# A fused attention and matrix-product kernel: the planner's list scheduling by due times replaced by a listed order of 2706 tasks

## The chip, the cores and the metric

One NeuronCore of a Trainium2 chip. Its engines are TensorE (PE; PEld is its weight load), VectorE (DVE), ScalarE (ACT), GpSimd (POOL) and SyncE (SP). Each takes its own instructions strictly in the order in which the program lists them, and waits on semaphores for the others. In this program SP and POOL issue the DMAs. The metric is device time in microseconds, the median of several runs.

## The reference

Softcapped attention of 4 batches by 12 heads, then four weight matrices:

```python
def _attn_ref(q, k, v, cap):                      # (4, 12, 448, 64) each
    scores = scale * np.matmul(q, k.transpose(0, 1, 3, 2))
    scores = cap * np.tanh(scores / cap)
    scores = scores - np.max(scores, axis=-1, keepdims=True)
    attn = np.exp(scores)
    attn = attn / (np.sum(attn, axis=-1, keepdims=True) + 1e-09)
    return np.matmul(attn, v)

def _moe_ref(x, w1, w2, w3, w_out):               # x (1792, 768), d_ff 1024
    a = x @ w1
    b = x @ w2
    h = a * b @ w3
    return h @ w_out
```

`x` is the attention's output, laid out as 1792 tokens by 768. The weights arrive as 64-bit floats.

## The kernel before

**How the work is cut.** The 48 heads are 24 pairs. For a pair `pr` there are three score tasks `S{pr}_1..3` (L501, six matmuls each), and for each two pairs a fourth, `S{pr}_0` (L488, the last 64 keys, on 64x64 tiles of the array). Behind each stands a tanh `H` (L514) and an exp `E` (L517) on ScalarE. `V{pr}_1..3` (L555, four 32-column tiles) and `VJ` (L571, 64x64 tiles) multiply by v; `A` adds exps on VectorE (L621, L623); `T` and `Y` (L638, L651) sum with a matrix of ones. `Q` and `O` copy sums and values out of PSUM (L700, L704), and `R0` to `R3` invert the sums by way of DRAM, `N0` scales and `N` stores the pair's result (L744, L747).

All matmul operands but those of V, T and the 64x64 tasks are split in a high and a low part, each product being three matmuls. A weight piece goes through `load`, `low`, `sign`, `top`, `join` (64-bit to 32-bit on ScalarE and VectorE: L280 or L275, L286, L270 or L263, L291), then `high` and `out` or `h` and `l`: a rounding cast on either engine (L297, L341) and a subtraction on VectorE (L300, L344). `h{pr}_0` and `l{pr}_0` do this for q and k (L447, L451).

`O` and `Z` pieces are w_out and w3. `C` (pc, L1233) forms w3 @ w_out, evacuated by `D` and stored by `DS`. `W` pieces are w1 and w2, combined by a seven-product scheme (L362, L876), their splits stored by `WS` (L905) for a second use. `X` tasks load, combine and split the attention's output (tiles x0T, x0B, x1T, x1B). `P` (pab, L1098, three matmuls of 448 columns) are the products with w1 and w2; `eM1`, `eU`, `eM5`, `eV` copy them from PSUM (L1067), other `e` tasks combine them (L1078), `U` stores a * b (L1084). In the last part `q` loads those, `s`, `ha`, `la` combine and split them (L1363, L1384, L1388), `p` (m, L1452, 384 columns) multiplies with w3 @ w_out, and `w` stores the result (L1497).

**The two parts.** All tasks of the first part (24 pairs, w_out, w3, w1, w2, half of the products) are put into a plan and run; then the attention's pools are closed, and a second part is planned in the freed space. Its first tile that needs that space is written by `X1_0_0h`, a cast on ScalarE.

**What sets the order.** `put` gives a task its engine, an estimated duration, a due time (key), its needs, and for casts, evacuations and some loads and stores a second engine (ACT or DVE; SP or POOL). `Plan.run` then builds the program: it repeatedly takes the engine that is free first, takes from its ready tasks the one with the smallest due time, and emits that task's instructions; an estimated price is charged when a matmul task leaves one tiling of the array (`form`: S, Q, T or none) for another. `SHIFTS` moves the due times of 670 tasks by hand-listed amounts. The order of emission is each engine's order, and it also decides which buffer of a pool a tile gets, since pools hand out their buffers in turn. Estimated times take no part on the chip: semaphores alone do.

A second copy of the program, for a cap above 32, is built behind a branch; with the reference's cap of 30 it is not run.

Of the kernel before, what the change touches and what calls it, by code (L numbers as in the profile page):

```python
# [37 lines left out]
class Slots:  # L38
# [9 lines left out]
    def close(self):  # L48
        self.uses[self.closed :] = sorted(
            self.uses[self.closed :], key=lambda x: (x[0] + x[2].shift, x[1])  # L50
        )
# [94 lines left out]
def program(  # L146
# [85 lines left out]
    def put(name, eng, ns, key, emit, needs=(), lat=0.0, alt=(), after=()):  # L232
# [725 lines left out]
    def plan_xprep(r):  # L958
# [54 lines left out]
        for kt in range(HX):  # L1013
# [19 lines left out]
        for kt in range(HX):  # L1033
# [484 lines left out]
    with tc.manual_schedule():  # L1518
# [82 lines left out]
ldv2:-27.24 h2_0:-53.64 l2_0:-89.4 ld3:-70.26 ldv3:-35.39 ld4:-54.83 ldv4:-11.34 ld10:13.08
h11_0:36.3 ld13:-4.51 h13_0:45.03 ld14:-12.57 h14_0:31.49 ld15:-21.06 h15_0:31.8 ld16:-26.21
h16_0:21.8 ld17:-29.77 h17_0:19.68 l17_0:-10.19 ld18:-23.1 h18_0:20.3 ld19:-49.03 h19_0:16.53
ld20:-27.06 h20_0:7.2 ldv21:38.57 h21_0:35.19 ld22:-35.21 ldv22:37.84 h22_0:68.74 ldv23:38.58
h23_0:66.31 S0_1:-192.79 H0_1:-187.63 E0_1:-55.03 S0_2:-186.95 H0_2:-147.89 E0_2:-137.57
S0_3:-148.33 H0_3:-146.59 S0_0:-185.75 H0_0:-120.74 E0_0:-75.64 S1_1:-143.99 H1_1:-57.11
S1_2:-127.09 H1_2:-54.85 S1_3:-128.32 H1_3:-15.3 Q0:-49.46 O0:-18.46 N00:-29.44 T1:2.67
S2_1:-82.53 S2_2:-127.98 S2_3:-84.68 S2_0:-88.56 H2_0:4.61 S3_1:-80.27 H3_1:7.89 S3_2:-74.1
S3_3:-63.27 H3_3:7.08 V2_1:-4.66 VJ3:-3.79 V3_1:18.59 Q3:-1.56 S4_1:-56.06 H4_1:4.39 S4_2:-47.38
H4_2:7.21 S4_3:-34.57 H4_3:3.21 S4_0:-40.96 E4_0:-32.07 S5_1:-34.49 S5_2:-27.33 S5_3:-15.47  # L1610
# [48 lines left out]
X0a10:-52.7 X0t10:-19.82 X0c00:-15 X0b10:-18.2 X0T30:1.52 X0_5_0h:24.07 X0a11:-20.2 X0c01:3.2
X0_1_1h:22.17 X0_2_1h:-32.27 X0T31:-3.78 X0_5_1l:-13.29 X0a12:-3.41 X0t12:-2.26 X0b12:-3.23  # L1660
X0T22:13.58 X0_4_2h:24.23 X0_4_2l:13.95 P0_0_0_1:16.8 P0_0_0_2:-2.08 eM1_0_0:-47.62
P0_0_1_1:-24.42 eU_0_0:-6.02 P0_0_4_0:80.3 eV_0_0:-13.5 P0_0_5_0:12.86 P0_1_2_0:13.26
eU_0_1:-17.16 P0_1_3_0:6.71 eV_0_1:-31.07 P0_1_5_0:4.02 P0_2_0_1:2.93 P0_2_1_0:-2.97
# [105 lines left out]
```

## Time and profile before

| | |
|---|---|
| median of 3 runs | 565.93 us (565.09 to 569.05) |
| the profiled execution | 567.21 us, of which the span from first to last instruction is 565.4 us |
| TensorE | busy 548.5 us (97%), 3660 matmuls |
| VectorE | busy 433.0 us (77%), 874 instructions |
| ScalarE | busy 342.6 us (61%), 545 instructions |
| GpSimd | busy 82.1 us (15%), 150 instructions, nearly all DMA issues |
| DMA | 131.08 MB, 232 GB/s in the mean |

A row of the trace gives the line of the kernel, the engine, the operation, and the tile written and those read (`pab<-x0T,wt`), with buffer numbers left out. Matmuls overlap, and their ends are modelled: the distance between two starts or two ends in a full stretch is what one costs, not its own duration.

### The profile page before, as it was taken

Reading aid. Unit: us, or ns where it says so; the run is one execution under the profiler, and the core shown is the slowest. Engines: PE = TensorE matmul, PEld = TensorE weight load, DVE = VectorE, ACT = ScalarE, POOL = GpSimd, SP = SyncE. Lnnn points to the kernel's source line nnn. Section 1 sums busy time; section 2 is a strip of 40 time slices with the busy share of each in tenths; the row PEclk is TensorE's granted clock in tenths of the full one; section 3 lists DMA queues with packets and bytes.
Section 4 is the critical chain, followed back from the end, with each engine's and each line's share of the span. In section 5 each row is a group of like instructions: output and inputs, shape, how many; then the busy total and the mean of one; then the engine's idle time right before and its main releaser. Section 6 shows DMA issues by size and latency. Waiting matters only on the chain.

```text
span 565.4 us, 10168 instructions
## 1 busy us (share of the span) xinstructions
PE 548.5 (97%) x3660; PEld 426.7 (75%) x3660; DVE 433.0 (77%) x874; ACT 342.6 (61%) x545; POOL 82.1 (15%) x150
## 2 busy tenths in 40 slices
PE   6999999999999999999999899999999999999994
PEld 3354558977576556667578889899999999999994
DVE  5998999687989999998987898765522676875531
ACT  6998998487978999887854654422211353344120
POOL 0000011101131111212213120111011001111311
PEclk9999999999999999999999999999999999999998
DMA  8678777758897876977579877899886233553311
GB/s 277 172 254 277 240 233 252 244 182 261 283 329 261 272 255 236 353 254 290 197 271 348 321 253 245 274 340 300 295 291 261 89 108 102 179 148 107 85 70 64
DMA packets 62510, 131.08 MB, mean 232 GB/s; under 512 B 12738, under 2 KB 40770, under 8 KB 60914
## 3 DMA queue, kind: packets, MB, share of 16 engines
q1 hardware_dynamic: 51746, 78.65, 44.2%
q0 software_dynamic: 10704, 51.68, 24.3%
q8 instruction: 31, 0.51, 0.4%
q14 instruction: 29, 0.24, 0.1%
HBM read 88.46 MB, written 41.77 MB: 230 GB/s over the span
## 4 chain that ended last, share of the span: by engine, by line
PE 73%; issue 9%; DVE 7%; DMA 5%; ACT 3%; POOL 1%; SPq 0%; POOLq 0%; DVEq 0%; ACTq 0%
PE pab L1098 35%; PE m L1452 13%; PE pv L555 7%; PE s L501 6%; PE pc L1233 6%; DMA r<-r_dr 3%; PE sum L638 2%; DMA r_dr<-z 1%; PE s L488 1%; PE pv L571 1%; PE sum L651 1%; ACT p L514 1%; POOL out_dram L1497 1%; DVE wt L344 1%; ACT p L517 1%
## 5 line engine op out<-in xcount | busy, mean ns | idle before, releaser
L517 ACT ACTIVATE p<-p,ncap_sb,acap_sb 128x896 f32<-128x896 f32 x84 | 92.6, 1138 | 0.1
L514 ACT ACTIVATE p<-s,tsc_sb 128x896 f32<-128x896 f32 x84 | 82.3, 1008 | 8.8 <-PE s L501 5.9
L1233 PEld LDWEIGHTS pc<-wo,w3t 128*128 128x128 f32 x384 | 65.6, 188 | 12.1 <-issue 5.9
L1233 PE MATMUL pc<-wo,w3t 128*128 128x384 f32 x384 | 73.3, 342 | 0.4 <-DVE wo L300 0.4
L1098 PE MATMUL pab<-x0T,wt 128*128 128x448 f32 x288 | 64.8, 371 | 2.4 <-ACT M L1067 2.3
L501 PE MATMUL s<-hl 64*128 64x448 f32 x432 | 58.9, 396 | 5.7 <-ACT hl L447 4.4
L1098 PE MATMUL pab<-x1T,wt 128*128 128x448 f32 x288 | 63.5, 368 | 0.1
L501 PEld LDWEIGHTS s<-hl 64*128 64x128 f32 x432 | 38.0, 190 | 33.6 <-ACT p L514 9.9
L555 PE MATMUL pv<-p,v 128*32 128x448 f32 x576 | 62.6, 546 | 0.6 <-ACT p L517 0.4
L1098 PEld LDWEIGHTS pab<-x0T,wt 128*128 128x128 f32 x288 | 52.8, 188 | 13.5 <-ACT M L1067 3.4
L1452 PE MATMUL m<-bT,ot 128*128 128x384 f32 x336 | 61.9, 334 | 0.0
L1452 PEld LDWEIGHTS m<-bT,ot 128*128 128x128 f32 x336 | 58.6, 188 | 0.1
L1098 PEld LDWEIGHTS pab<-x1T,wt 128*128 128x128 f32 x288 | 53.9, 188 | 5.8 <-ACT U L1067 0.4
L1098 PE MATMUL pab<-x0B,wt 128*128 128x448 f32 x216 | 48.7, 370 | 0.0
L1098 PE MATMUL pab<-x1B,wt 128*128 128x448 f32 x216 | 48.2, 368 | 0.0
L1452 PE MATMUL m<-bB,ot 128*128 128x384 f32 x252 | 47.1, 334 | 0.0
L1098 PEld LDWEIGHTS pab<-x0B,wt 128*128 128x128 f32 x216 | 39.7, 188 | 7.2 <-issue 1.7
L1384 ACT CAST ot<-A 128x512 fp32r<-128x512 f32 x40 | 23.6, 621 | 35.1 <-DVE A L1363 27.7
L1452 PEld LDWEIGHTS m<-bB,ot 128*128 128x128 f32 x252 | 44.0, 188 | 0.0
L1098 PEld LDWEIGHTS pab<-x1B,wt 128*128 128x128 f32 x216 | 40.5, 188 | 4.1
L1067 ACT COPY M<-pab 128x448 f32<-128x448 f32 x27 | 14.3, 531 | 39.4 <-PE pab L1098 39.2
L555 PEld LDWEIGHTS pv<-p,v 128*32 128x32 f32 x576 | 15.5, 109 | 28.8 <-issue 18.6
(143 smaller groups left out, 801.7 us busy)
## 6 DMA issues: line engine op xcount, KB each, us to landing
raw_w<-in_moe_w_dram SPq DMA_DIRECT2D x48, 384.0 KB
w_dr<-wt POOLq DMA_DIRECT2D x42, 384.0 KB, 4.5
wt<-w_dr POOLq DMA_DIRECT2D x10, 1536.0 KB, 7.7
kq<-in_kq_dram SPq DMA_DIRECT2D x23, 450.0 KB
raw_wo<-in_moe_w_out_dram SPq DMA_DIRECT2D x16, 384.0 KB
A<-u_dr SPq DMA_DIRECT2D x24, 256.0 KB
v<-in_v_dram SPq DMA_DIRECT2D x24, 224.0 KB
r<-r_dr SPq DMA_DIRECT2D x48, 112.0 KB
```

What stands on the lines that cost most here:

```text
L344: nc.vector.tensor_tensor(dst(1), src(), dst(0), op=ALU.subtract)
L488: nc.tensor.matmul(box[0][quarter(pr + n, j), n, :S], lhsT=raw_t[pr + n][at, QO + S + KM :], rhs=raw_t[pr + n][at, QO : QO + S], start=Tru ...
L501: nc.tensor.matmul(box[0][:, j, :S], lhsT=hl[at, a, S + (i - 1) * P : S + i * P], rhs=hl[at, c, :S], start=(z == 0), stop=(z == 2),)
L514: nc.scalar.activation(p, box[0][:, :, :S], AF.Tanh, scale=tsc_sb)
L517: nc.scalar.activation(p_t[pr, i], p_t[pr, i], AF.Exp, scale=acap_sb, bias=ncap_sb)
L555: nc.tensor.matmul(pv_t[pr][n * 32 : (n + 1) * 32, :S], lhsT=v_t[pr][:, 3 * j + i - 1, g * 32 : (g + 1) * 32], rhs=p_t[pr, i][:, j, :], st ...
L638: nc.tensor.matmul(box[1][n * 32 : (n + 1) * 32, :SH], lhsT=ones[:, :32], rhs=part[:, j, g * SH : (g + 1) * SH], start=(x == 0), stop=(x = ...
L1067: cp(ev[name], box[bank][:, :S])
L1098: nc.tensor.matmul(box[bank][:, :S], lhsT=w_op(r, m, i)[:, a, kt, :], rhs=xt[r, i][:, kt, c, :S], start=(new and kt == 0 and z == 0), stop ...
L1233: nc.tensor.matmul(box[0][:, :NH], lhsT=w3t[n][:, a, jt, :], rhs=wo[jt][:, c, ns], start=(jt == 0 and z == 0), stop=(jt == KF - 1 and z == 2),
L1384: copy(ot[j][:, q % 3, 0], ru[src])
L1452: nc.tensor.matmul(box[banks[m]][:, :NH], lhsT=ot[q // 3][:, q % 3, a, k, :], rhs=bt[RHS[m]][:, k, c, :], start=(new and k == 0 and z == 0 ...
```

## The change

`Plan.run` no longer orders the main program. A text, `SEQUENCE`, names all 2706 tasks in order, 1663 before a bar and 1043 behind it (the planner of before put 1655 and 1051 into its two parts; the bar closes the attention's pools, as the end of the first part did). A name alone means the task's first engine; `/DVE`, `/ACT` or `/POOL` names its second. The tasks themselves, their instructions and their operands are the same. `SHIFTS` is removed. A need of one of the planner's tasks (T2) is corrected, for the general program, which alone is still planned.

```diff
-            self.uses[self.closed :], key=lambda x: (x[0] + x[2].shift, x[1])
+            self.uses[self.closed :], key=lambda x: (x[0], x[1])
...
-            t.key = (t.key + t.shift, i)
+            t.key = (t.key, i)
...
-    shifts = {} if general else {
-        x.split(":")[0]: float(x.split(":")[1]) for x in SHIFTS.split()
-    }
+    part = iter(SEQUENCE.split("|"))
+
+    def run(goals):
+
+        if general:
+            plan.run(goals)
+            return
+        for x in next(part).split():
+            name, _, eng = x.partition("/")
+            opts = done[name].opts
+            opts[eng or next(iter(opts))][1]()
...
-            total("T2", kt, "t1", "b1", "t1", key, [f"X{r}b1{kt}", f"X{r}T1{kt}" if r and kt else f"X{r}t1{kt}"])
+            total("T2", kt, "t1", "b1", "t1", key, [f"X{r}b1{kt}", f"X{r}_{op('T1')}_{kt}l" if r and kt else f"X{r}t1{kt}"])
...
-        plan.run(goals)
+        run(goals)
...
-SHIFTS = """
-ld0:-93.52 ldv0:-52.56 h0_0:-137.13 ld1:-66.82 ldv1:-42.73 h1_0:-55.2 l1_0:-66.93 ld2:-66.42
...
+SEQUENCE = """
+ld0 O0_0load ld1 O0_1load ldv0 ld2 O1_0load ldv1 h0_0/DVE l0_0 h0_1 cap S0_1 l0_1 H0_1 S0_2 O0_0low
+O0_0sign H0_2 O0_0top S0_3 O0_0join E0_1 h1_0/DVE O2_0load S0_0 O0_1low l1_0 H0_3 ld3 V0_1 O0_1top
...
+W6A11join P0_4_4_1 W6A21join W7A11load P0_4_4_2 N022 P0_4_3_2 N023 N22 eV_0_4 W5S4 N23 P0_4_6_0
+eM5_0_4 W6A12low/ACT P0_4_6_1 W5_5h W6A12sign P0_4_5_0 W6_0h/DVE W5_2l P0_4_6_2 W6S3 P0_4_5_1 |
+X1b00 X1a00 X1a02 WS5_3 X1a01 eu0_0_4 P0_4_5_2 W5_5l U0_4 P0_5_1_0 eo12_0_4 P0_5_1_1 X1b01 W6S1
+W7A12load P0_5_0_0 eo22_0_4 X1_0_0h WS5_4 W6A12top P0_5_0_1 WS5_2 W6_0l P0_5_0_2 W6S2 P0_5_1_2
+W6A12join eM1_0_5 X1_0_0l W7A11low/ACT P0_5_2_0 W6_2h W7A11sign P0_5_2_1 W6_3h eo11_0_5 P0_5_2_2
...
+p6_3_2 p6_6_3 p6_3_3 e6U p6_2_1 e612 p6_2_2 e6V w6o12 p6_4_0 e622 p6_2_3 p6_4_1 w6M5 e611/DVE
+p6_4_2 w6o11/POOL p6_4_3 e621 w6U
```

Against the order that the planner of before emits, task for task: 135 tasks move from ScalarE to VectorE and 69 the other way; 106 DMA tasks move from POOL to SP and 7 the other way. By engine, before and after: PE 876 and 876; VectorE 841 and 907; ScalarE 544 and 478; SP 303 and 402; POOL 142 and 43. The kind of tiling changes 156 times along the matmul tasks of before, 115 times along those of the list.

## Rows read from the trace of the kernel before

**Rows 1.** The page: busy us, share and instructions; busy tenths in 40 slices.

```profile
PE 548.5 (97%) x3660; PEld 426.7 (75%) x3660; DVE 433.0 (77%) x874; ACT 342.6 (61%) x545; POOL 82.1 (15%) x150
...
PE   6999999999999999999999899999999999999994
```

**Rows 2.** Stretches: us, busy us and instructions by engine, granted clock, DMA share, GB/s.

```profile
0.00:80.00 80.00, 74.32 (x672) 37.11 (x673) 67.98 (x165) 72.98 (x95) 3.03 (x9) 1.00 0.77 244
...
80.00:200.00 120.00, 118.16 (x919) 84.54 (x918) 106.89 (x225) 97.66 (x150) 20.39 (x37) 1.00 0.79 260
...
200.00:320.00 120.00, 118.44 (x832) 81.04 (x831) 108.59 (x214) 91.44 (x143) 24.96 (x42) 1.00 0.78 278
```

**Rows 3.** Chain that ended last: start us, us, engine, tile, line, instructions.

```profile
50.84 0.72 PE pc L1233 x3
...
54.79 1.14 PE sum L638 x24
...
89.62 17.90 PE pc L1233 x102
...
201.43 2.39 PE pv L555 x24
...
205.23 0.91 PE pv L571 x8
...
206.15 1.41 PE s L501 x12
...
207.55 0.81 PE pab L1098 x3
...
219.07 0.80 PE s L501 x6
...
226.96 0.89 PE pv L555 x8
...
358.83 92.02 PE pab L1098 x444
...
461.53 69.18 PE m L1452 x399
```

**Rows 4.** Timeline, first 30 us: start, us, engine, line, operation [idle before, releaser].

```profile
4.40 0.74 PE L501 MATMUL s<-hl 64*128 64x448 f32 x2 [4.40 <-ACT hl L447]
...
10.00 0.36 DVE L275 TENSOR_SCALAR raw_wo<-raw_wo 128x384 int32<-128x384 int32 x1 [2.97 <-DMA raw_wo<-in_moe_w_out_dram]
...
24.77 0.96 PE L555 MATMUL pv<-p,v 128*32 128x448 f32 x8 [0.45 <-ACT p L517]
```

**Rows 5.** Timeline, three later places where TensorE waited.

```profile
176.76 0.67 PE L501 MATMUL s<-hl 64*128 64x448 f32 x4 [1.04 <-DVE hl L451]
...
198.11 1.09 PE L1098 MATMUL pab<-x0T,wt 128*128 128x448 f32 x4 [0.77 <-ACT M L1067]
...
312.12 0.57 ACT L341 CAST x1B<-xs1a 128x448 fp32r<-128x448 f32 x1 [3.02 <-issue]
...
315.49 0.86 PE L1098 MATMUL pab<-x0T,wt 128*128 128x448 f32 x3 [1.54 <-ACT M L1067]
```

**Rows 6.** Lines by shape: count, busy us, mean ns, idle before.

```profile
L270 ACT ACTIVATE t_w<-raw_w 128x384 f32<-128x384 f32 x35 | 19.1, 561 | 0.3 <-DVE wt L344 0.2
...
L263 DVE TENSOR_SCALAR t_w<-raw_w 128x384 f32<-128x384 f32 x13 | 4.5, 349 | 0.0
...
L341 ACT CAST wt<-t_w 128x384 fp32r<-128x384 f32 x32 | 15.4, 512 | 10.5 <-DVE t_w L291 5.3 <-PE pab L1098 3.6 <-DVE t_w L362 1.5
...
L341 DVE CAST wt<-t_w 128x384 fp32r<-128x384 f32 x16 | 5.5, 350 | 0.5 <-PE pab L1098 0.5
```

**Rows 7.** DMA: the page's issues, lines by shape, SP's timeline and SP's waits.

```profile
w_dr<-wt POOLq DMA_DIRECT2D x42, 384.0 KB, 4.5
...
L905 POOL DMA_DIRECT2D w_dr<-wt x42 | 24.0, 571 | 80.2 <-DVE wt L344 64.3 <-issue 7.6 <-ACT U L1067 3.4
...
308.89 0.32 SPq L905 DMA_DIRECT2D w_dr<-wt  x1
...
SPq L1084 <- DVE M L1078: 35.4, 5, 20.1
```

**Rows 8.** Timeline, end of the span.

```profile
556.01 1.73 PE L1452 MATMUL m<-bB,ot 128*128 128x384 f32 x9
...
558.43 0.55 POOL L1497 DMA_DIRECT2D out_dram<-U  x1
```

More of the change, by code (lines that the diff above doesn't have):

```diff
@@ L1590, in program @@
             plan_out(t)
-        plan.run(goals)
+        run(goals)
 CAP_MAX = 32.0
-SHIFTS = """
-ld0:-93.52 ldv0:-52.56 h0_0:-137.13 ld1:-66.82 ldv1:-42.73 h1_0:-55.2 l1_0:-66.93 ld2:-66.42
[L1601 to L1610, printed above, removed]
@@ L1659 @@
[L1659 to L1663, printed above, removed]
-P0_2_4_0:4.59 P0_2_5_0:4.14 P0_2_6_0:-40.94 P0_3_0_0:2.54 P0_3_1_1:17.44 P0_3_2_0:2.86
@@ new lines @@
+S3_2 O2 ldv4 E3_1 R21 O2_1out T2 O4_0load Z0_2low O3_1high/DVE ld6 Z0_2top/ACT Y2 Z0_2sign H3_2
+O2_0out V3_1 N00 E3_3 S4_2 Z0_1high/DVE N0/POOL Z0_2join S4_1 O3_1out Q2 Z0_1out H4_2 R02 C0_1_2
+O3_0low O6_0load C0_0_1 O3_0top H4_1 O3_0sign R31 C0_0_2 O4_0top C0_1_3 E3_2 h5_0/DVE O3_0join S4_0
+O4_0low E4_2 O5_0load l5_0 S4_3 E4_1 O4_0sign V3_2 R12 H4_0 V3_3 O4_0join R22 O6_0low T3
+Z0_2high/DVE O3 N01 ldv5 Y3 O5_1load O6_0sign H4_3 N1/POOL V4_1 O6_0top h6_0/DVE Q3 S5_1 E4_3
+O6_0join R03 O3_0high/DVE S5_2 O4_0high/DVE O4_1load E4_0 O3_0out V4_2 R32 O5_0low O4_0out H5_2
@@ new lines @@
+V4_3 l6_0 ld7 O5_0top/ACT C0_0_3 O5_0sign E5_2 C0_0_4 O5_0join VJ5 R13 H5_1 O7_0load O5_1low R23
+S6_1 O4_1top O4 ldv6 O5_0high/DVE S5_3 E5_1 O4_1low O5_1sign T4 N02 O5_1top/ACT V5_1 N2 H5_3
+O5_1join O4_1sign V5_2 Z1_0load H6_1 O5_0out X0a00 Y4 h7_0/DVE E5_3 S6_2 O4_1join S6_3 Z0_2out
+O6_1load O5_1high/DVE H6_2 O7_0low V5_3 O5_1out Q4 O7_0sign E6_1 R04 S6_0 O7_0top ldv7 O6_0high/DVE
+O7_0join O5 ld8 T5 l7_0 E6_2 O7_1load Y5 R33 V6_1 Z1_0low H6_3 O7_0high/DVE O6_0out V6_2
+O4_1high/DVE H6_0 Z1_0top S7_1 O4_1out O6_1low/ACT Z1_0sign S7_3 O6_1top/ACT R14 Z1_0join E6_3
@@ new lines @@
+E13_3 Z7_1out R011 S14_1 ldv13 W0A12top R110 E13_2 S13_1 W0A12low R210 W1A12top C6_0_2 X0t10 W0S1
+Z7_2high H14_1 C6_1_2 W0S2 C6_0_3 Z7_2out W1A12low/ACT W0A12sign C6_1_3 h15_0 C6_1_4 W0A12join R310
+W1A12sign C6_0_4 H13_1 W1A11low C6_1_5 DS2_1 W1A12join C6_0_5 E13_1 R111 W1A22load C6_0_6 W1A11sign
+C6_1_6 W1A11top/ACT R211 W1A21load C6_0_7 W1A11join DS4_1 C6_1_7 W0_2h/DVE D6_0 A12_3 W0_6h VJ13
+X0_3_0h X0_3_0l V13_1 O12 D6_1 N010 X0b10 T12 X0_3_2h DS6_1/POOL W0_1h/DVE V13_2 ldv14 W1_1h A13_2
+Y12 X0_3_2l S14_3 Q12 W0_3h R012 A13_3 S14_2 X0c00 R311 h16_0 C7_0_0 l15_0 V13_3 H14_2 N10 W1A22low
@@ new lines @@
+W0_1l T13 H14_3 W1A22sign Y13 WS0_1/POOL l16_0 S14_0 W1_0h R112 S15_1 ld17 H14_0 W1_1l ldv15 C7_1_0
+N011 DS5_0 X0_3_1h C7_0_1 W2A11load W0_3l Q13 H15_1 R212 C7_1_1 X0T30 WS0_3/POOL N11 C7_0_2 X0_3_1l
+W1A21low/ACT R013 C7_1_2 W0S4 E14_1 X0c01 C7_0_3 X0T20 ld18 C7_0_4 W0_5h/DVE X0_1_0h W1A21sign
+C7_1_3 E14_2 X0_1_0l C7_1_4 X0_2_0h/DVE C7_0_5 W0_6l E14_3 C7_1_5 X0T40 C7_1_6 X0_2_0l O13 C7_0_6
+X0_4_0h A14_2 X0b11 C7_1_7 E15_1 R312 C7_0_7 X0_4_0l S15_2 D7_0 X0_5_0h/DVE X0a12 R113 E14_0 S15_3
+W1A21top R213 W0_2l V14_1 H15_2 X0_6_0h/DVE X0_6_0l V14_2 E15_2 X0_5_0l X0t11 V14_3 A14_3 X0a11
@@ new lines @@
+X0_5_1h WS1_1 VJ15 H15_3 W1A21join R313 X0T31 S16_1 O14 W0_5l WS0_2 E15_3 S16_3 W1A22top DS6_0 N012
+ldv16 T14 H16_1 V15_1 W2A12load A15_2 Y14 X0_1_2h V15_2 D7_1 A15_3 Q14 H16_3 V15_3 R014 X0T21 N12
+T15 X0_1_1h X0_5_1l Y15 X0_2_1h X0_1_1l S16_2 X0b12 X0_4_1h X0_2_1l E16_1 S16_0 X0_4_1l N013 h17_0
+X0t12 P0_0_0_0 W1S3 ldv17 P0_0_0_1 Q15 X0_1_2l H16_2 R015 P0_0_1_0 X0T41 WS0_0 P0_0_0_2 H16_0
+W2A12low X0c02 R114 P0_0_1_1 W1_0l eM1_0_0 R214 P0_0_1_2 l17_0 E16_0 ld19 P0_0_2_0 WS0_6 eo11_0_0
+W2A11low/ACT P0_0_2_1 X0T22 O15 P0_0_3_0 E16_3 R115 P0_0_3_1 W2A12sign R215 h18_0/DVE E16_2
@@ new lines @@
+X1_0_1h/DVE P0_5_3_2 W5_6l WS5_5/POOL W6_1l P0_5_4_0 eM5_0_5 X1_0_1l P0_5_4_1 W7A11top P0_5_4_2
+W6S4 W7A11join P0_5_5_0 eV_0_5 X1_0_2l W7A22load P0_5_5_1 W6_6h X1T12 W6_5h P0_5_6_0 W6_2l X1a10
+P0_5_5_2 W7A12low XT10 X1T11 P0_5_6_1 X1c00 eo12_0_5 P0_5_6_2 X1b10 W7A12sign WS5_6 P0_6_0_0
+eu0_0_5 WS6_1 W7A22top/ACT P0_6_0_1 X1_3_0h/DVE W7A22low/ACT W6_3l P0_6_0_2 W6_4l P0_6_1_0
+W7A12top/ACT eM1_0_6/DVE X1t10 W7A21top/ACT P0_6_1_1 eo22_0_5 WS6_0 W7A21low/ACT P0_6_1_2 W7A22sign
+eu1_0_5 P0_6_2_0 eo11_0_6 P0_6_2_1 U1_5 W7A12join P0_6_3_0 X1T30 P0_6_3_1 W6_5l X1_4_0h P0_6_3_2
@@ new lines @@
+P1_7_3_2 w1g1/POOL X1_6_2l P1_7_4_1 eM5_1_7 bT1_0 P1_7_4_2 bB11_1h X1_5_2l bT1_0h P1_7_5_0 bT3_0
+eV_1_7 X1_6_1l P1_7_5_1 bT3_0h P1_7_6_0 bT3_0l bT1_0l P1_7_5_2 bc11_2_0 bB11_1l P1_7_6_1 eo12_1_7
+P1_7_6_2 bT1_1 P1_0_0_0 eu0_1_7 bT1_1h P1_0_0_1 bT1_1l U2_7/POOL P1_0_0_2 bT2_1 w1g2/POOL bT2_0
+P1_0_1_0 eM1_1_0 bT3_1 P1_0_1_1 bT2_0h bc21_0_0 bc21_1_0 bT3_1h/DVE P1_0_1_2 bT3_1l P1_0_2_0
+eo11_1_0 P1_0_2_1 eo22_1_7 P1_0_2_2 P1_0_3_0 eU_1_0/DVE P1_0_3_1 eu1_1_7 P1_0_3_2 U3_7 P1_0_4_0
+eM5_1_0/DVE w1g3 P1_0_4_1 bc12_2_0 P1_0_5_0 P1_0_4_2 P1_0_5_1 eV_1_0 P1_0_5_2 bB11_2h P1_0_6_0
@@ new lines @@
+eo12_1_0 P1_0_6_1 bT2_1h/DVE P1_1_0_0 P1_0_6_2 P1_1_0_1 eu0_1_0 P1_1_0_2 eo22_1_0 U2_0/POOL
+P1_1_1_0 bT4_0 eM1_1_1 bT2_1l w1g4/POOL P1_1_1_1 bT2_0l P1_1_2_0 bT4_1 bc22_2_0 P1_1_1_2 q0A11
+P1_1_2_1 eo11_1_1 q0A21 P1_1_2_2 P1_1_3_0 eU_1_1/DVE P1_1_3_1 bB11_2l eu1_1_0 P1_1_4_0 P1_1_3_2
+U3_0 P1_1_4_1 bc21_2_0 eM5_1_1/DVE P1_1_4_2 bT1_2 bT4_0h/DVE P1_1_5_0 eV_1_1 w1g5 bT4_0l P1_1_5_1
+bT1_2h q0A22 eo22_1_1 bT4_1h P1_1_6_0 bT3_2 P1_1_5_2 bT3_2h P1_1_6_1 eo12_1_1 P1_1_6_2 bT1_2l
+P1_2_0_0 eu0_1_1 P1_2_0_1 bT3_2l U2_1 P1_2_1_0 bc11_3_0 P1_2_0_2 bc12_3_0 P1_2_1_1 eM1_1_2 P1_2_1_2
```

227 lines of the change are left out of this document (146 added, 81 removed).

## Prediction

> **What bounds the kernel now.** I read the page first, for the busy shares and the forty slices; then the stretches, to see whether one engine limits everywhere; then the chain of work that ended last, for the price of a matmul in a full stretch and just behind another kind; then the timeline where TensorE's idle time has a named releaser.
>
> The page says TensorE [rows 1]: 548.5 of 565.4 us busy, every slice but the first and last at 8 or 9 tenths, at a granted clock of 1.00 (2.4 GHz) in every stretch [rows 2]. Matmul ends are modelled, so "busy" hides two things the reader is to see: time lost in changing the tiling of the array, and short waits. The chain shows the first [rows 3]. A projection matmul (pab) in a run of 444 costs 92.02/444 = 0.207 us, but three behind another kind take 0.81, not 0.62: 0.19 for the change. Likewise: pc 17.90/102 = 0.1755, three behind another kind 0.72: 0.19. Scores (s): a second task of six adds 1.41 - 0.80 = 0.61, so the first carries 0.19. Values (pv): (2.39 - 0.89)/2 = 0.75 per task, the change 0.14. The 64x64 tasks always stand between other kinds (0.91); I take 0.17 of that, the mean of the other prices, an estimate.
>
> With these the time can be taken apart. TensorE runs from 4.40 us [rows 4] to 556.01 + 1.73 = 557.7 [rows 8]: 553.3 us. Matmuls alone: 1008 pab x 0.207 = 208.9; 588 m x (69.18/399) = 101.9; 384 pc x 0.1755 = 67.4; 72 score tasks x 0.61 = 43.9; 72 value tasks x 0.75 = 54.0; 480 sum matmuls x (1.14/24) = 22.8; 24 of the 64x64 tasks x 0.74 = 17.8. Together 516.7. In the order of before, the kind changes 156 times: 23 times into pc, 18 into pab (0.19 each), 43 into scores (0.19), 48 into values or sums (0.14), 24 into 64x64 (0.17): 4.4 + 3.4 + 8.2 + 6.7 + 4.1 = 26.8. The rest, 553.3 - 516.7 - 26.8 = 9.8 us, is waiting. Three waits of it lie late: 1.04, 0.77 and 1.54 [rows 5]; most of the others lie in the first 80 us, where ScalarE (72.98 of 80) and VectorE (67.98) are nearly full too [rows 2].
>
> So TensorE's own stream is the bound, and an order can win at most part of 26.8 + 9.8.
>
> **The change part by part.**
>
> *The order of the matmuls.* No matmul is added or removed. I counted the changes of kind along the listed tasks: 115 instead of 156. Into pc 13 (10 fewer), pab 10 (8 fewer), scores 39 (4 fewer), values and sums 32 (16 fewer), 64x64 21 (3 fewer): 1.9 + 1.5 + 0.8 + 2.2 + 0.5 = 6.9 us saved. All at 0.14 would be 5.7, all at 0.19 7.8: these are the bounds. 17 of the 41 lie among the first 100 matmul tasks (61 changes, now 44): 2.9 us in the first 80, 4.0 later. Value 6.9.
>
> *Casts moved from ScalarE to VectorE.* 135 tasks move there, 69 move back: net 66. A move is a piece's top from 561 to 349 ns, or a cast from 512 to 350 [rows 6], so ScalarE loses some 66 x 0.53 = 35 us of busy time and VectorE gains some 66 x 0.35 = 23. Early this matters. Up to the last exp of head pair 7, ScalarE's list shrinks from 88 to 79 tasks; beside tanh, exp and the two copies per pair it holds 10 instead of 18. That takes 8 x 0.5 = 4 us out of the engine for which values wait at 24.77. In the first microseconds h0_0 goes to VectorE ahead of the cap's scalars, and the first raw w_out load moves up from sixth to second on SP, so the 2.97 us that VectorE lost waiting for it falls away [rows 4]. Against that, VectorE takes the moved work where it has 12 us of 80 free. Between "the 4 us reach TensorE" (-4) and "VectorE is late instead" (+1.5) I take -1.2, nearer to nothing, because VectorE is at 85% there [rows 2].
>
> *The three late waits.* At 313 us: ScalarE stood in x1B's first cast (3.02 idle, then 312.12), the copy of M queued behind it, and TensorE waited for the copy [rows 5]. That cast writes a buffer whose space the attention pools hold until the last store of pair 23, which GpSimd issued. In the list N23 is issued by SP, and nine matmul tasks stand between it and that cast instead of seven (1.2 us more), so I expect the wait to shrink, not to go. At 176 us the scores of pair 15 waited for l15_0; four matmul tasks stand between them now, instead of two, but the sum T13 has only three behind its addition A13_3 instead of nine. At 198 us the copy eM1_0_0 was late; one matmul task stands behind it instead of none. Together 3.35 us; bounds -3.35 and 0; value -1.2, a third.
>
> *DMA issues.* 106 tasks move from GpSimd to SP and 7 the other way: SP issues 402 of 445 tasks instead of 303, GpSimd 43 instead of 142. An issue costs SP 0.32 us where it cost GpSimd 0.57 [rows 7]; SP gets 99 x 0.34 = 34 us more of issuing over 565, hidden since it feeds nothing but itself. What isn't hidden is order: on SP a store that waits for its data holds every load listed behind it. The price is with the rivals. At the end the last store, w6U, goes from GpSimd (issue 0.55, [rows 8]) to SP (0.32): -0.2, bounds 0 and -0.6.
>
> The Trainium skill, DMA: Bandwidth & Descriptors (Specifications), gives a first byte after about 1 us for GpSimd's path and 0.6 for SP's; by it N23 would land 0.4 us sooner. No row here shows a landing on SP's queue beside GpSimd's 4.5, so the sum stands without it.
>
> *What falls to nothing.* Sorting buffers and computing due times happen when the program is built; no instruction. The corrected need of T2 is read by the planner alone, which now runs only for the general branch; that branch is skipped at cap 30. If the cover failed it would cost that whole second program, which the trace of before doesn't run either.
>
> *New waits.* The stream gets 7 us shorter, so the other engines have that much less time, and VectorE goes from 106.9 and 108.6 busy of 120 [rows 2] to some 111 and 113. New short waits have no row; bounds 0 and +7 (all the saving refilled); I take +2.3, a third.
>
> **Sum.** -6.9 - 1.2 - 1.2 - 0.2 + 2.3 = -7.2 us. On the span: 565.4 to 558.2. The profiled execution took 567.2, 1.3 more than the median of 565.93, and would come to 560.0; the median to 558.7 us.
>
> **Rivals.**
>
> 1. *VectorE is the real limit up to 320 us.* For: 283.5 us busy of 320 [rows 2], 89%, and it gets some 6 us more of work there (566 tasks in the first part instead of 545). If its idle time stays what it is, the matmuls before 320 us, where every change of kind lies, can't come sooner, and only the last store and half a wait remain: -1 to -3, some 564 (the sum of half a wait, 0.8, the last store, 0.2, and up to 2 that VectorE's shorter idle time gives). Against: part of its idle time is waiting for others, such as the 2.97 us at the start [rows 4], and the list removes some of that.
>
> 2. *SP's queue holds the loads: slower.* For: before, SP already stood 35.4 us in five waits for u0's data, 20.1 in the longest [rows 7], and 67 of the moved tasks are stores of split weights, products and heads that will stand ahead of loads. If a weight or x load comes late by a landing, 4.5 us [rows 7], a whole row of matmuls waits. Two such cancel the gain; three make 558.7 + 13.5 = 572.2, slower by 1%. Against: stores stand in the list right behind what they store, so each waits briefly if that is on time, and loads are listed several tasks ahead. From the third held load on this decides.
>
> The Trainium skill speaks for this rival: Perfetto Trace Analysis (DMA Optimizations) advises balancing issues across engines and keeping inputs on one and outputs on another. The list does the opposite. That page's premise is a queue full of issuing; here 402 tasks at 0.32 us [rows 7] are 129 us, under a quarter of the span.
>
> 3. *The list is the old order in another form.* Excluded: 204 compute tasks and 113 DMA tasks change engine, and 41 changes of kind go.
>
> **How the numbers follow.** Forecast (shorter stream, about as much waiting): 0.61, own range 553.5 to 561. Rival 1: 0.29, 560.5 to 566. Rival 2 with a full price: 0.10, 566 to 580. A tenth of the forecast's share could fall below 553.5, when the waits go as well (-6.9 - 4 - 3.4 = 551.6). The range 553 to 566 leaves out about 0.06 below and 0.12 above. One per cent, about what a measurement of this kernel tells from no change, is 560.3 and 571.6. The forecast lies below 560.3 but for a small part (0.03): faster 0.58. Rival 1, that part and half of rival 2 lie within: 0.37. Slower: the other half, 0.05, the case of three held loads or more.
>
> **What the profile after would show.** GpSimd's busy time falls to 43 x 0.57 = 25 us, ScalarE's to about 308, VectorE's rises to about 456; 3660 matmuls as before. The first matmul starts within 0.5 us of 4.4, the last ends near 550. In the stretch 80:200 more matmuls fit than 919. If rival 1 holds, VectorE is over 95% busy up to 320 us and TensorE's waits name it. If rival 2 holds, TensorE or the casts wait for DMA loads and SP shows long waits at stores (L905, L747, L1084). Wrong would be: fewer changes of kind and yet the same length of stream before 320 us with no waits named, for then the price of 0.14 to 0.19 isn't one of the change.

## The result and the profile after

The changed kernel takes 552.21 us in the median (551.51 to 554.15, 4 runs), where the kernel before took 566.1 beside it: a ratio of 0.9752, 95% interval 0.9707 to 0.9797. A later comparison on one chip gave 553.03 us and 0.9733 (0.9703 to 0.9762). It is faster, by nearly twice what was forecast: 552.2, where 558.7 was expected and 553 was the lower end of the range. Its profiled execution took 551.55 us, its span 549.8 (before: 567.21 and 565.4). Line numbers of the new kernel are those of before plus 7.

The page, busy us by engine and the tenths of TensorE, beside [rows 1]:

```profile
PE 538.0 (98%) x3660; PEld 430.4 (78%) x3660; DVE 454.7 (83%) x940; ACT 310.6 (56%) x479; POOL 25.4 (5%) x49
...
PE   6999999999999999999999999999999999999995
```

As many matmuls as before, 10.5 us less busy time for them, no slice at 8 tenths any more between the first and the last. ScalarE lost 32 us, VectorE gained 22, GpSimd went from 82 to 25.

The same three stretches as [rows 2]:

```profile
0.00:80.00 80.00, 75.46 (x718) 41.83 (x718) 72.33 (x179) 72.90 (x92) 1.93 (x6) 1.00 0.77 245
...
80.00:200.00 120.00, 119.61 (x942) 86.88 (x939) 109.36 (x229) 100.69 (x151) 3.26 (x6) 1.00 0.82 257
...
200.00:320.00 120.00, 119.95 (x824) 88.38 (x822) 115.22 (x237) 84.15 (x135) 7.02 (x13) 1.00 0.85 294
```

TensorE stands 0.39 us in 80:200 and 0.05 in 200:320, where it stood 1.84 and 1.56. It does so although VectorE is 96% busy in the last of them. The waits of TensorE, in total, times, longest, are two:

```profile
PE s L508 <- DVE hl L454: 4.4, 1, 4.4
...
PE pab L1105 <- DVE M L1085: 0.4, 1, 0.4
```

The first is the wait for the first q and k; of the later waits only this one of 0.4 us is named.

**Where the time went.** To compare runs I took every trace apart in one way. For each matmul task the distance from its start to the next one's start is known; I subtracted the undisturbed distance of its kind (0.52 us for a task of pc or m, 0.62 for pab, 0.61 for scores, 0.75 for values and the 64x64 tasks, 0.38 for eight sum matmuls) and, at a change of kind, its price (the prediction's 0.14 to 0.19, parted into what comes before and behind the change). What is left is waiting. So the column of changes is a count times the prediction's prices and no measurement of its own; that the stretches without a wait come out near zero by them, and the fourth experiment, are what speaks for the prices. The tail is from the end of the last matmul to the end of the span. In us of the profiled execution (its own time is up to 2.2 us off its kernel's median):

| kernel | median | changes of kind | waits 0 to 80 | waits 80 to 320 | from 320 on | tail | span |
|---|---|---|---|---|---|---|---|
| before | 566.1 | 156: 26.4 | 6.0 | 4.6 | 0.6 | 7.6 | 565.4 |
| after | 552.21 | 115: 19.6 | 3.7 | 1.3 | -1.5 | 6.6 | 549.8 |
| after, once more | 553.03 | 115: 19.6 | 3.7 | 1.1 | 0.1 | 6.8 | 551.1 |
| issuers as before | 553.13 | 115: 19.6 | 4.1 | 1.8 | -1.5 | 7.3 | 551.4 |
| casts' engines as before | 562.14 | 115: 19.6 | 5.6 | 8.5 | -1.6 | 7.7 | 559.8 |
| start as before | 558.01 | 130: 22.2 | 5.1 | 4.0 | -1.3 | 6.7 | 556.9 |
| 24 changes more | 557.61 | 139: 23.9 | 4.0 | 1.2 | -1.6 | 7.2 | 554.6 |
| 135 casts to ScalarE | 569.50 | 115: 19.6 | 7.2 | 16.4 | -1.7 | 7.4 | 569.3 |
| 69 casts to VectorE | 560.69 | 115: 19.6 | 3.6 | 9.2 | 0.0 | 6.7 | 559.0 |
| 7 changes fewer | 558.51 | 108: 18.5 | 9.2 | 2.7 | 0.3 | 7.9 | 558.5 |
| 9 changes fewer | 564.09 | 106: 18.1 | 8.8 | 8.0 | -1.3 | 7.9 | 561.5 |
| before, list's issuers | 570.91 | 156: 26.4 | 6.2 | 7.5 | 3.6 | 7.4 | 571.2 |
| before, list's casts' engines | 579.59 | 156: 26.4 | 7.5 | 13.4 | 3.7 | 7.4 | 578.3 |
| before, list's start | 584.71 | 141: 23.7 | 4.1 | 25.8 | 2.9 | 7.7 | 584.1 |

The -1.5 is no wait: some executions ran pab faster there (last section). So I compare waits up to 320 us, and the whole by the second trace of after, whose pab runs as before's. There 14.3 us of span went, by this division: 6.8 with the changes of kind, 5.8 with waits before 320 us, 0.5 behind, 0.8 in the tail, 0.3 at the first matmul.

### The profile page after: what moved, and what is told of

Same layout as the page of the kernel before. It is cut to its first block, busy times and chain, and to the rows that moved or that the text cites. A ratio compares the mean times of both kernels' runs of the same rounds, so it can differ in the third digit from the quotient of the medians.

```text
span 549.8 us, 10088 instructions
## 1 busy us (share of the span) xinstructions
PE 538.0 (98%) x3660; PEld 430.4 (78%) x3660; DVE 454.7 (83%) x940; ACT 310.6 (56%) x479; POOL 25.4 (5%) x49
## 4 chain that ended last, share of the span: by engine, by line
PE 93%; DMA 3%; ACT 1%; DVE 1%; SPq 0%; issue 0%; ACTq 0%
PE pab L1105 37%; PE m L1459 19%; PE pc L1240 13%; PE pv L562 9%; PE s L508 9%; PE sum L645 3%; PE pv L578 2%; PE s L495 2%; PE sum L658 2%; DMA v<-in_v_dram 1%; DMA r_dr<-z 1%; ACT p L524 1%; DMA kq<-in_kq_dram 1%; DMA w_dr<-wt 1%; ACT p L521 1%; DVE M L1085 0%
## 5 line engine op out<-in xcount | busy, mean ns | idle before, releaser
L524 ACT ACTIVATE p<-p,ncap_sb,acap_sb 128x896 f32<-128x896 f32 x84 | 94.1, 1139 | 0.4
L1240 PE MATMUL pc<-wo,w3t 128*128 128x384 f32 x384 | 70.4, 339 | 0.0
L1459 PE MATMUL m<-bT,ot 128*128 128x384 f32 x336 | 67.8, 334 | 0.0
L508 PE MATMUL s<-hl 64*128 64x448 f32 x432 | 57.3, 393 | 4.4 <-DVE hl L454 4.4
L1459 PE MATMUL m<-bB,ot 128*128 128x384 f32 x252 | 52.4, 334 | 0.0
L1391 ACT CAST ot<-A 128x512 fp32r<-128x512 f32 x26 | 15.5, 621 | 38.5 <-DVE A L1370 20.9
L562 PEld LDWEIGHTS pv<-p,v 128*32 128x32 f32 x576 | 16.6, 109 | 24.2 <-issue 14.9
```

The lines of the kernel that those rows point to most:

```text
L508: nc.tensor.matmul(box[0][:, j, :S], lhsT=hl[at, a, S + (i - 1) * P : S + i * P], rhs=hl[at, c, :S], start=(z == 0), stop=(z == 2),)
L524: nc.scalar.activation(p_t[pr, i], p_t[pr, i], AF.Exp, scale=acap_sb, bias=ncap_sb)
L562: nc.tensor.matmul(pv_t[pr][n * 32 : (n + 1) * 32, :S], lhsT=v_t[pr][:, 3 * j + i - 1, g * 32 : (g + 1) * 32], rhs=p_t[pr, i][:, j, :], st ...
L1240: nc.tensor.matmul(box[0][:, :NH], lhsT=w3t[n][:, a, jt, :], rhs=wo[jt][:, c, ns], start=(jt == 0 and z == 0), stop=(jt == KF - 1 and z == 2),
L1391: copy(ot[j][:, q % 3, 0], ru[src])
L1459: nc.tensor.matmul(box[banks[m]][:, :NH], lhsT=ot[q // 3][:, q % 3, a, k, :], rhs=bt[RHS[m]][:, k, c, :], start=(new and k == 0 and z == 0 ...
```

## The experiments

Each kernel is the listed one, or the one before written as a list, with some tasks moved or given another engine; a task without a suffix has its usual engine. The edits are shown by their first tokens. Experiments 5 to 8 ran on another chip than 1 to 4 and 9 to 12; the kernel before took 566.1 to 567.4 us in the median in all of them, so amounts between kernels are good to about a microsecond.

**1. Issuers as before.** All 113 DMA tasks that changed queue go back.

```
-N2 N3 DS0_1 DS0_0 ... w6U
+N2/POOL N3/POOL DS0_1/POOL DS0_0/POOL ... w6U/POOL
```

> The listed order with the DMA issuers of before: 106 tasks back from SP to GpSimd and 7 from GpSimd to SP, each at its place in the list. Theory (the gain is 6.8 us of changes of kind and 7.6 us of waits, most of them VectorE's, ScalarE's and the first loads'): the issuer matters at two places alone, the store N23 before the second part's first cast (up to 1.5 us of waiting back) and the last stores (about 1 us): 552.9 to 554.7 us; no other named wait of TensorE. Rival (the issuer is what took the waits away): waits come back in many places, 556 to 560 us. Rival (SP's queue holds loads in the listed order): GpSimd's issuing makes it faster, under 551 us.

553.13 us (551.81 to 553.7), ratio 0.9743 (0.9704 to 0.9782): the issuers are worth a microsecond at most. The tail is 0.7 longer, one wait of 1.09 us came at 179 us. The wait of TensorE at x1B did not come back, though N23 is GpSimd's again and ScalarE's cast stands waiting for it:

```profile
302.84 0.57 ACT L348 CAST x1B<-xs1a 128x448 fp32r<-128x448 f32 x1 [4.92 <-DMA x_dr<-xf]
```

**2. Casts' engines as before.** The 204 casts and copies that changed engine go back, order and issuers stay.

```
-h0_0/DVE Z0_0low O1_1high/DVE Z0_0high/DVE Z0_1top ...
+h0_0 Z0_0low/ACT O1_1high Z0_0high Z0_1top/ACT ...
```

> The listed order with the ScalarE/VectorE choice of before for all 204 casts and copies that had moved, each at its place in the list. Theory: ScalarE is again full in the first 80 us, waits of 2 to 4 us come back there and hardly any later: 554 to 557 us. Rival (VectorE is the limit up to 320 us): 66 tasks fewer on VectorE make it the same or faster, 549 to 552.5 us.

562.14 us (561.73 to 562.37), ratio 0.9908 (0.9872 to 0.9944), 9 to 10 us of the gain gone. That is beyond both forecasts, and not in the first 80 us, where I had put it: of the 9.1 us more waiting up to 320 us, 7.2 lie behind 80. The stretch 200:320, and the largest wait (timeline):

```profile
200.00:320.00 120.00, 116.70 (x809) 82.55 (x806) 109.16 (x216) 88.54 (x143) 7.04 (x13) 1.00 0.83 282
...
219.99 0.96 PE L562 MATMUL pv<-p,v 128*32 128x448 f32 x8 [1.46 <-ACT p L524]
```

VectorE has 6 us less to do than in the listed kernel, and TensorE stands 3.3 us instead of 0.05. So VectorE's busy time is not what bounds the listed kernel in this stretch: less of it was slower.

**3. The start as before.** The tasks up to V7_3 (some 80 us) stand in the order and on the engines of before, the rest is the list's: 130 changes of kind.

> The tasks that the list places up to V7_3 (about the first 75 us) in the order and on the engines of before, the rest as listed. 130 changes of kind instead of 115. Theory (what the start loses is lost, TensorE being the bound behind it): 15 x 0.17 = 2.6 us of changes of kind and some 2.5 us of waits come back: 556.5 to 558 us. Rival (another engine is the bound later, and a late start is caught up): 552.2 to 554 us.

558.01 us (557.6 to 558.77), ratio 0.9832 (0.9795 to 0.9868). Of 7.1 us of span 2.6 are changes of kind, 1.4 waits before 80 us, 2.7 waits behind the seam, most of it at 80 to 100 us. The list's start is worth 5 to 6 us, though the seam has a part in it.

**4. More changes of kind.** 12 pc and pab tasks are taken out of their runs and put between tasks of one other kind: 24 changes, no wait wanted.

```
-C0_1_0 C0_1_1 C0_0_0 ... T2 Y2
+C0_1_0 C0_0_0 ... T2 C0_1_1 Y2
```

> The list with 12 projection or w3 matmul tasks put between two score, value or sum tasks of one kind: 139 changes of kind instead of 115, nothing else moved. Theory (a change of kind costs 0.14 to 0.19 us and nothing hides it): 24 x 0.17 = 4.1 us more, 555.3 to 557 us, with the named waits about as they are. Rival (the changes are hidden in waits for other engines): 552 to 553.2 us.

557.61 us (556.55 to 560.24), ratio 0.9842 (0.9799 to 0.9886). The matmuls end at 547.43 instead of 543.12: 4.31 us for 24 changes, 0.18 each, where 0.17 was expected (the median lies a little above the 555.3 to 557 expected); waits up to 320 us are 5.2, as they were (5.0). So nothing hides a change, and the price is of the size that the chain gave.

**5. The casts' engines alone, in the order of before.** The counterpart of the second.

> The order of before, with the 204 casts and copies on the engine that the list gives them. 156 changes of kind. Theory (the assignment itself relieves ScalarE, in any order): waits of the first 80 us and of 175 to 315 us shrink, 558 to 563 us. Rival (assignment and order are a pair: each cast was given the engine that is early at its place in the list, and out of that place it is late): as putting the old casts into the list cost 10 us, putting the new casts into the old order costs 2 us or more, 567 to 576 us.

579.59 us (578.91 to 581.09), ratio 1.0226 (1.0172 to 1.028). What saves 10 us in one order costs 13 in the other; the waits go from 11.2 to 24.6, spread over scores, values, sums and pab. Order and engines are one choice, not two that add up. The loss is larger than even the rival's range said, and no run tells which of the moves makes it.

**6. The start of the list, the rest as before.**

> The tasks up to V7_3 as listed, with the list's engines, and everything behind them in the order and on the engines of before. 141 changes of kind instead of 156. Theory (start and rest add up: the old start cost the list 5.8 us): 15 x 0.17 = 2.6 us of changes and 2 to 3 us of waits go, 560 to 562 us. Rival (the rest's own waits, or VectorE's work up to 320 us, take the time back): 564 to 567 us.

584.71 us (583.54 to 586.03), ratio 1.0308 (1.0253 to 1.0363). The stretch 80:200, and TensorE's two longest waits:

```profile
80.00:200.00 120.00, 108.45 (x779) 78.68 (x780) 91.43 (x192) 80.23 (x125) 17.42 (x32) 0.92 0.67 217
...
PE pc L1240 <- DVE wo L307: 9.0, 1, 9.0
PE pc L1240 <- DVE w3t L304: 6.7, 1, 6.7
```

The old rest reaches for pieces of w_out and w3 that the old start would have had ready and the new one has not: 15.7 us at the seam. I had expected a gain of 4 to 6 us. The run says nothing of what the start is worth, and I draw nothing on that from it.

**7. Only the 135 moves to VectorE undone.** These go back to ScalarE, the 69 in the other direction stay as listed.

> The listed order with only the 135 casts and copies that had gone from ScalarE to VectorE given back to ScalarE; the 69 that went the other way stay on ScalarE. ScalarE then holds 613 tasks. Theory (ScalarE's queue is what makes the waits): the 10 us of the run with all 204 reverted come back or more, 562 to 568 us, with waits named after ScalarE. Rival (VectorE is the limit up to 320 us): the same or faster than the list, 549 to 553 us.

569.50 us (568.71 to 571.15, 10 runs), ratio 1.0053 (1.0025 to 1.0082): 17 us lost, half a per cent slower than the kernel before, and more than the 562 to 568 expected. ScalarE is busy 106.1 of 120 us in 80:200 and 98.2 in 200:320, so it is not full either. What happens is seen at V18_3, whose exp is E18_3 (timeline of this kernel, then of the listed one at the same task):

```profile
224.93 0.55 ACT L348 CAST wt<-t_w 128x384 fp32r<-128x384 f32 x1
225.33 0.59 ACT L1074 COPY M<-pab 128x448 f32<-128x448 f32 x1
225.76 0.62 ACT L277 ACTIVATE t_w<-raw_w 128x384 f32<-128x384 f32 x1
226.22 1.06 ACT L521 ACTIVATE p<-s,tsc_sb 128x896 f32<-128x896 f32 x1
227.11 1.19 ACT L524 ACTIVATE p<-p,ncap_sb,acap_sb 128x896 f32<-128x896 f32 x1
228.35 1.12 PE L562 MATMUL pv<-p,v 128*32 128x448 f32 x8 [2.02 <-ACT p L524]
```

```profile
211.21 0.34 DVE L348 CAST wt<-t_w 128x384 fp32r<-128x384 f32 x1
211.48 0.60 DVE L1074 COPY M<-pab 128x448 f32<-128x448 f32 x1
212.01 0.34 DVE L270 TENSOR_SCALAR t_w<-raw_w 128x384 f32<-128x384 f32 x1
212.93 1.15 ACT L524 ACTIVATE p<-p,ncap_sb,acap_sb 128x896 f32<-128x896 f32 x1
213.34 1.74 PE L562 MATMUL pv<-p,v 128*32 128x448 f32 x16
```

Three small operations (W1_6h, eM1_0_1 and W2A21top) stand on ScalarE ahead of a tanh and an exp that the matmuls need; the list has them on VectorE, and V18_2 and V18_3 follow each other without a wait (the last line). Their 1.3 us (224.93 to 226.22) are most of the 2.02 that the values then wait. This is one wait followed to its cause; the others I read only from their named releasers.

**8. Only the 69 moves to ScalarE undone.** The mirror image.

> The listed order with only the 69 casts and copies that had gone from VectorE to ScalarE given back to VectorE, which then holds 976 tasks (some 69 x 0.3 = 21 us more, of which VectorE has about 21 free up to 320 us). Theory (VectorE has room, since its 115 busy of 120 us between 200 and 320 us left TensorE no named wait): 552 to 554.5 us. Rival (VectorE is the limit up to 320 us, just not reached by the list): 557 to 570 us, with VectorE over 97% busy and TensorE waiting for it.

560.69 us (560.61 to 560.94), ratio 0.9891 (0.9842 to 0.994): some 8 us lost. I had expected room; there was none. VectorE, third number of each stretch, and the first waits:

```profile
80.00:200.00 120.00, 117.86 (x931) 85.64 (x931) 116.36 (x255) 84.50 (x116) 3.27 (x6) 1.00 0.81 253
200.00:320.00 120.00, 115.48 (x799) 82.69 (x795) 117.36 (x248) 72.17 (x107) 7.31 (x13) 1.00 0.82 277
...
PE sum L645 <- DVE a L630: 2.1, 2, 1.8
PE pab L1105 <- DVE U L1074: 1.8, 1, 1.8
```

At 116.4 and 117.4 of 120 VectorE is named in all of TensorE's waits; at the list's 109.4 and 115.2 it was, behind the first wait, in one of 0.4 us. So VectorE can become the limit, as the first rival had it, and the list stays below that. Whether it is the sum of its work or, as in the seventh experiment, what stands ahead of a needed operation, this run does not part.

**9. Seven changes of kind fewer.** 24 matmul tasks of the listed order move by up to three places, so that short runs of one kind join.

```
-S0_0 V0_1 S1_1 S1_2 V0_2 ... S2_1 S2_3 V1_3 T1 Y1 ...
+S0_0 S1_1 S1_2 V0_1 V0_2 ... V1_3 T1 Y1 S2_1 S2_3 ...
```

> The listed order with 7 changes of kind fewer (108 instead of 115): 24 matmul tasks of the first 320 us stand up to three places from where the list has them, so that seven short runs of one kind join their neighbours; engines and all other orders are the list's. Theory (the price of a change of kind, some 0.15 us, is real in both directions, and the list's other tasks leave a swap of two or three matmul tasks room): the end of the matmuls comes 1.07 us sooner than the list's 543.1, some 551.1 us, waits unchanged near 3.5. Rival (the list's order is fitted to when the data come, so that any swap brings waits): the saving is eaten, 552 to 555, with waits named at the swapped tasks.

558.51 us (557.67 to 560.5), ratio 0.9834 (0.9805 to 0.9863). By the division the changes cost 1.1 less and the waits up to 320 us are 6.9 more: 5.5 us slower than the listed kernel beside it. TensorE's waits behind the first:

```profile
PE s L508 <- ACT p L521: 1.9, 4, 0.5
PE pv L562 <- ACT p L524: 1.3, 1, 1.3
PE sum L645 <- ACT xf L711: 1.1, 2, 0.7
PE s L495 <- ACT p L521: 1.0, 2, 0.5
```

They are short and many, and all name ScalarE's work on scores and values. A delay of a score task by two or three tasks (0.61 to 0.75 us each, so some 1.2 to 2.3) is more than the order has to spare.

**10. Nine fewer**, with two swaps more, by up to six places.

> As the kernel with 7 fewer, with two larger swaps more (106 changes of kind; 39 matmul tasks moved, by up to six places): the scores of pair 9 and those of pairs 18 and 19 go past five tasks of another kind. Theory: 1.45 us sooner than the list by the price of a change, some 550.8 us, if six places still leave room. Rival (fitted order): later scores bring later sums, waits of 1 to 3 us behind them, 552 to 556.

564.09 us (562.65 to 566.5, 12 runs), ratio 0.9938 (0.9917 to 0.9958): the two further swaps save 0.4 us of changes and cost 5 us of waits, more than half of it at 200 to 220 us, where two score tasks of pairs 18 and 19 stand six places later. Both kernels speak for the rival: the order is fitted to when the data come.

**11. The list's issuers in the order of before.**

```
-N2/POOL N3/POOL DS0_0/POOL ... w6U/POOL
+N2 N3 DS0_0 ... w6U
```

> The order and the casts' engines of before, with the list's issuers for the DMAs: 99 net issues go from GpSimd to SP, nothing else. Theory (the issuers are worth about 1 us, at the end of the program and at single waits; no load is held): 564.5 to 566, the same as before, with the last store 0.5 to 0.8 us sooner after the last matmul than before's 7.64. Rival (SP's queue holds loads when the stores stand in it): 568 to 580, with waits of TensorE or of the casts named after SP's queue.

570.91 us (566.94 to 573.09, 10 runs), ratio 1.0049 (1.0021 to 1.0077): some 3 us slower, where I had expected no change. One place of it is at 333 us. SP's queue in this kernel, and the same x load in the kernel before:

```profile
333.06 0.32 SPq L912 DMA_DIRECT2D w_dr<-wt  x1
333.43 0.42 SPq L981 DMA_DIRECT2D xs1t<-t_dr  x1
333.96 0.40 SPq L912 DMA_DIRECT2D w_dr<-wt  x1
334.41 0.49 SPq L981 DMA_DIRECT2D xs1a<-x_dr  x1
```

```profile
327.02 0.41 SPq L974 DMA_DIRECT2D xs1a<-x_dr  x1
```

Stores of split weights, GpSimd's before, now stand among the x loads, and this load comes 7.4 us later, in a stream that was only 2.9 us behind at the wait before (318.39 against 315.49). What SP waited at these stores in the whole run, before and here:

```profile
SPq L905 <- DVE wt L344: 6.3, 6, 2.5
SPq L912 <- DVE wt L351: 25.7, 21, 3.4
```

Behind such loads x casts wait, and the copies that TensorE needs wait behind the casts, at two places:

```profile
340.19 0.57 ACT L348 CAST x1B<-xs1a 128x448 fp32r<-128x448 f32 x1 [2.76 <-DMA xs1a<-x_dr]
341.71 2.12 PE L1105 MATMUL pab<-x0T,wt 128*128 128x448 f32 x9 [0.92 <-ACT V L1074]
...
351.06 0.56 ACT L348 CAST x1B<-xs1b 128x448 fp32r<-128x448 f32 x1 [2.50 <-DMA xs1b<-x_dr]
352.11 2.09 PE L1105 MATMUL pab<-x0T,wt 128*128 128x448 f32 x9 [1.47 <-ACT U L1074]
```

In the kernel before no cast of x on ScalarE waits for such a load. That is the prediction's second rival, in the order that it was not meant for. Which single store held which load was not tried.

**12. The changed kernel once more**, beside the two with fewer changes.

> The changed kernel itself, beside the two kernels with fewer changes of kind on the same chip, for a comparison at the level of a microsecond: 551.5 to 552.5, waits near 3.5, tail 6.6, 115 changes of kind.

553.03 us (551.33 to 553.41), ratio 0.9733 (0.9703 to 0.9762). No kernel that I tried beats it.

## Why the prediction was right in direction and too small

**The bound** was right: TensorE's own stream, with changes of kind and short waits in it. By the finer division above it was 26.4 and 11.2 us, where the prediction had 26.8 and 9.8.

**Changes of kind: -6.9 forecast, -6.8 by the division.** That is the same count at the same prices, so the agreement proves nothing by itself. Independent of it is the fourth experiment: at its 0.18 us each, 41 changes are 7.4 us. The Trainium skill, TensorEngine Tiling (Key Properties), says that a change of tiling mode drains TensorE. The traces agree in so far as each change costs 0.14 to 0.19 us.

**New waits: +2.3 forecast, none left in the balance; and the moves of casts costed for the start only. This is the step that failed.** I reasoned that a stream 7 us shorter leaves the other engines less time and that a third of the saving would be refilled. I had costed the 204 reassignments as a sum of busy time (35 us off ScalarE, 23 onto VectorE) and given them an effect in the first 80 us alone; behind that they stood at nothing, without a reason. The runs showed the waits up to 320 us fall from 10.6 to 5.0, and the reassignments take part in that over the whole stretch. In the list's order with the old engines (the second experiment) these waits are 14.1 us, 3.5 more than before; whether because the stream is shorter or because this order was made for other engines, no run parts. Both halves of the move are needed: without the 135 the waits up to 320 us are 23.6, without the 69 they are 12.8, with both 5.0. What they change is not which engine is the fuller, but whether a cast stands ahead of an exp, a sum or a copy that TensorE needs next; that was followed through at one wait (V18_3), and is argued for the rest. The order of emission also decides which buffer a tile gets; no run held that apart, but it is the same in the second experiment, so it alone does not take the waits out.

**The start: -1.2 forecast, -2.3 measured** (waits 0 to 80: 6.0 to 3.7), within its bounds. The value wait at 24.77 [rows 4] is gone; what remains lies in the first 15 us.

**The three late waits: -1.2 forecast, -3.3 measured** for all waits at 80 to 320 (4.6 to 1.3), close to the bound of -3.35: the second term that was too small. At x1B I expected the wait to shrink for two reasons, the store on SP and two matmul tasks more in between. It went, and the first experiment excludes the store. The cast itself stands even longer than before, against [rows 5], now for a load:

```profile
297.96 5.03 PE L1105 MATMUL pab<-x0B,wt 128*128 128x448 f32 x24
301.66 0.57 ACT L348 CAST x1B<-xs1a 128x448 fp32r<-128x448 f32 x1 [4.81 <-DMA xs1a<-x_dr]
302.42 0.53 ACT L1074 COPY M<-pab 128x448 f32<-128x448 f32 x1 [0.20 <-DMA xs1a<-x_dr]
303.01 2.34 PE L1105 MATMUL pab<-x0T,wt 128*128 128x448 f32 x10
```

ScalarE stands 4.81 us instead of 3.02, but a run of 24 matmuls covers it, and TensorE loses 0.17 us by the division above, where it lost 1.68. What is left of the two reasons is the distance between the tasks; that is argued by elimination, no run moved those tasks alone.

**The end: -0.2 forecast, -0.8 to -1.0 measured.** Against [rows 8]:

```profile
541.40 1.73 PE L1459 MATMUL m<-bT,ot 128*128 128x384 f32 x9
543.16 0.56 DVE L1490 TENSOR_TENSOR U<-U,m 128x384 f32<-128x384 f32 x1 [1.01 <-PE m L1459]
543.74 0.33 SPq L1504 DMA_DIRECT2D out_dram<-U  x1
```

The issue ends 0.94 us behind the last matmul (544.07 - 543.13), before 1.24 (558.98 - 557.74): 0.3 for the issuer, near the forecast. The rest is the landing, 5.7 us here and 6.4 before; with the same store on the same queue it was 6.9 in the ninth experiment, so I don't count it as a gain of the change.

**The rivals.** The first gave as its sign VectorE over 95% busy up to 320 us and waits that name it. The busy time came in the last of the three stretches (96%), the waits did not; the eighth experiment shows them at 97 to 98%. The Trainium skill, Perfetto Trace Analysis (Optimizing Scalar/DVE Operations), says that with VectorE saturated it may make sense to offload work to ScalarE. By that the 135 moves are the wrong way. At VectorE's 115 of 120 giving them back cost 17 us; at 117 the advice fits, since the 69 moves to ScalarE save some 8. The second rival, SP's queue, stayed out: the eleventh experiment shows that it is real in the old order (some 3 us) and the first that in the list it costs TensorE less than a microsecond, though there too ScalarE stands 4.81 us for an x load. The Trainium skill, Perfetto Trace Analysis (DMA Optimizations), says that it may help to balance DMAs across engines where issuing is the bottleneck, and to part inputs from outputs; in the old order the issuers of before, which keep to this more nearly, are some 3 us faster than the list's, and in the listed order they are not faster.

**The checks named ahead.** GpSimd 25.4 busy (25 forecast), ScalarE 310.6 (308), VectorE 454.7 (456), 3660 matmuls, 942 in 80:200 (over 919), the first at 4.35 (4.4). Only the end of the last differed, 543.1 instead of 550.

**The sum.** -6.9 - 1.2 - 1.2 - 0.2 + 2.3 was -7.2. In its place stand -6.8 - 2.3 - 3.3 and some -0.9 at the end, with nothing for new waits: -13.3. The new waits make 2.3 of the 6.1 us between the two sums, the late waits 2.1, the start 1.1 and the end 0.7. The rest of the 14.3 of the second trace lies behind 320 us and at the first matmul. The range's lower end, 553, left 6% below it; the case in which "the waits go as well" (551.6) was worked out and held for too unlikely.

## What to carry to other kernels

Where an engine's in-order stream is the bound, count its changes of tiling and price them from the chain of the trace; that part of a reordering can be forecast to about half a microsecond (6.9 forecast, 7.4 at the price of the fourth experiment). What waits it leaves can't be read from the busy shares of the helping engines: look, task by task, at what stands ahead of the operation that the bound engine needs next, and judge order and engine choice together, since either alone was slower here than both. A reassignment of work is therefore to be costed over the whole stretch in which it is made, not only where an engine is full. A fitted order has no slack to spend: the order with seven changes of tiling fewer saved 1.1 us of changes and brought some six times that in waits.

## What the runs showed of the hardware

**One run of matmuls, two paces.** The long run of pab took these times in two executions of the same kernel, the changed one (the chain that ended last):

```profile
338.65 98.77 PE pab L1105 x486
```

```profile
337.97 100.69 PE pab L1105 x486
```

0.2032 and 0.2072 us a matmul, at a granted clock shown as 1.00 in both; before it was 0.2072 [rows 3]. By the distance of starts a task of three takes 0.608 or 0.620 us, and most of that run goes at the faster pace in ten of the fourteen traces. Both paces also occur within one execution: in the second of these two, 0.608 from 321 to 337 us and 0.620 from 340 on, and in the eleventh experiment 0.620 from 367 to 413 and 0.608 behind it. Many of the changes, not all, come where a wait of a few tenths interrupted the run. The cause is open; it is 1.9 us of time that no order gave.

**The clock and idle time.** In the sixth experiment TensorE stood for 6.7 us up to 80.63 and for 9.0 us up to 97.25, and the granted clock was 0.92 in the mean of 80:200 and 1.00 in 200:320. In stretches of 5 us it was 0.50 (1.2 GHz) in 80:85 and in 95:100, where the two waits end, and 1.00 (2.4 GHz) again in 105:110. Nine pc matmuls took 3.61 us at 80.63, and 1.84 in the listed kernel at 24.88, at a clock of 1.00. So a long wait there cost more than its own length. In no other run did one of these stretches fall below 0.99.
